# k projections of two heads as one 128-row matmul, and a projection buffer of two single banks, in a fused attention and feed-forward kernel

## The chip, the cores and the metric

The kernel runs on one core of a Trainium2 chip. The metric is the device time of one execution in microseconds (us). The engines are TensorE (PE; its weight loads are listed as PEld), VectorE (DVE), ScalarE (ACT), GpSimd (POOL) and SyncE (SP), which here issues all DMAs in one queue. PSUM, where matmuls write, has eight banks; a bank holds 512 float32 per partition.

## The reference

Linear attention with an exponential feature map, and a two-layer feed-forward network (FFN) on its result, all in float32:

```python
batch, n_heads, seq, head_dim = (8, 8, 576, 64)      # d_feat = 128
def phi(x):
    proj = np.einsum('bhsd,df->bhsf', x, w_phi)
    proj = proj - np.max(np.abs(proj), axis=-1, keepdims=True)
    return np.concatenate([np.exp(proj), np.exp(-proj)], axis=-1)
q_p, k_p = (phi(q), phi(k))
kv = np.einsum('bhsf,bhsd->bhfd', k_p, v)
z = np.sum(k_p, axis=2)
num = np.einsum('bhsf,bhfd->bhsd', q_p, kv)
den = np.einsum('bhsf,bhf->bhs', q_p, z)[..., None] + 1e-06
x = (num / den)                                       # 8 x 576 = 4608 tokens of 512
h = x @ w_in                                          # 512 x 2048
g = 0.5 * h * (1.0 + erf(h * inv_sqrt2))
return g @ w_out                                      # 2048 x 512
```

## The kernel before, in words

The program does not write its instructions down in the order in which they run. Each function calls `op(...)` with an engine, a cost, the buffers read and written, and a rank; `Plan.order` then plays the engines against each other by these costs, takes on each engine the ready operation of lowest rank, and keeps track of buffer slots, activation tables, DMA and PE's clock; `emit` issues everything in the order of the planned starts. So a changed cost, a changed number of slots or a changed kind moves instructions on all engines. On the chip every engine works off its own queue in that order and waits by semaphores. For PE, `SHAPE` says which kinds of matmul use the array in the same division ("f" FFN, "k", "q" projections, "v" kv sums, "n", "d" numerators), and `BEHIND` and `BEFORE` are the costs at a change of division.

**Attention.** Eight batches. `k_quad(b, g, ...)` treats four heads: two pairs of head rows are stacked on 128 partitions (kt), 576 keys of the two pairs lie in nine chunks of 128 columns. The chunks go in five units, of 2, 2, 1, 2 and 2. For each unit, PE projects the chunk (pk): a matmul for each half of 64 partitions, each 64 rows by 128 columns, into the two banks of the pk tile. DVE takes the largest absolute value (mx) and subtracts it in place, ACT makes both exponentials (ek), and PE adds the products with v (vt) in kv, which ACT copies to kvn. `q_pair` projects half a sequence of two heads (pq, two matmuls with 64 rows), ACT copies it (pc), POOL reduces over partitions (mb), DVE subtracts, ACT makes the exponentials (ef), PE makes the numerators (pn), ACT copies them (xo), and DMA writes them to memory (x_d). For batches 0 and 1 the denominators come from PE as a 65th column; for the others DVE (un) and POOL (db) form them. `quotients` makes the reciprocals (dc).

**Buffers in PSUM.** `PS = dict(pp=1, kv=1, pn=1, ph=2, po=1)`: pp is one slot of two banks for pk and, from batch 2 on, for pq. The first two batches (`EB`) take pk from pp and po in turn (`EARLY_PK`) and pq from ph.

**Weights.** 32 tiles of w_in and w_out arrive as 64-bit floats; DMA, two ACT and five DVE instructions for each make of it a high and a low float (raw, wt, w).

**FFN.** 18 blocks of 256 tokens. DMA fetches x_d (xr) and the reciprocals (rb), DVE makes xr, xh and xl; eight steps u each make 24 matmuls with 256 columns (ph), two Gelu on ACT (gh, ph), a difference on DVE (gl) and 12 matmuls with 512 columns (po). Gelu and the exponential need different activation tables, so ACT loads a table when it changes between them.

The planner holds the FFN back until `TF = 90`. After the first block has started, PE works on FFN steps and on attention of later batches in turn.

Of the kernel before, what the change touches and what calls it, by code (L numbers as in the profile page):

```python
# [58 lines left out]
class Plan:
# [19 lines left out]
    def op(self, eng, cost, fn, r=(), w=(), also=(), rank=0.0, table=None, late=0.0, kb=0, duty=1.0, kind="f"):  # L79
        o = Op()  # L80
        o.eng, o.cost, o.fn, o.rank, o.table, o.late, o.n = eng, cost, fn, rank, table, late, len(self.ops)
        o.users, o.ready, o.nbytes, o.duty, o.kind = [], self.since, kb, duty, kind
# [20 lines left out]
        return o

    def order(self, bias):
# [162 lines left out]
def fused_kernel(ctx: ExitStack, tc: tile.TileContext, qT, kT, va, w_st, w_in, w_out, out):  # L268
# [17 lines left out]
    def mm(*a, **kw):  # L286
        return tc.keep_in_program_order(nc.tensor.matmul(*a, **kw))  # L287
# [78 lines left out]
    def k_quad(b, g, kvs, rank):  # L366
# [18 lines left out]
        for u, (p, cs) in enumerate(units):  # L385
            n = len(cs)
            mx = sb["mx"]([P, 2, n], F32, f"mx_{nm}_{u}")
            x = ps[EARLY_PK[turn[0] % len(EARLY_PK)] if b < EB else "pp"]([P, 2, 512], F32, f"pk_{nm}_{u}")
# [8 lines left out]
            xs = lambda x=x, n=n: x()[:, :, : n * NF].rearrange("p j (i f) -> p j i f", i=n)  # L397

            def proj(x=x, cs=cs):
                return [mm(x()[:, j, i * NF : (i + 1) * NF], lhsT=kt()[64 * j : 64 * j + 64, c * P : (c + 1) * P], rhs=wst()[64 * j : 64 * j + 64],  # L400
                           start=True, stop=True) for i, c in enumerate(cs) for j in range(2)]
# [3 lines left out]
                out=mx(), in_=xs(), axis=AX.X, op=ALU.max, apply_absolute_value=True), r=[x], w=[mx], **k())  # L405
            tt("dve", dve(256 * n, True), xs, xs, lambda mx=mx, n=n: mx().unsqueeze(3).to_broadcast([P, 2, n, NF]), ALU.subtract, [x, mx], [x], **k())
            for s in (1, 0):
                op("act", act(256 * n, True), lambda xs=xs, es=es, s=s: nc.scalar.activation(  # L408
                    es[s](), xs(), AF.Exp, scale=1.0 - 2.0 * s), r=[x], w=[e[s]], table="exp", **k())
# [129 lines left out]
    def block(j, rank):  # L539
# [25 lines left out]
        for u in range(NU):  # L565
# [101 lines left out]
def _layout(q, k, v, w_phi, moe_w_in, moe_w_out):  # L667
# [32 lines left out]
```

## Time and profile before

| what | value |
|---|---|
| time, median of 3 runs | 1154.89 us (1153.27 to 1155.93) |
| the profiled execution | 1153.51 us, span 1151.7 us, mean granted clock of PE 0.991 |
| PE busy / weight loads | 1111.6 us (97%) / 914.0 us |
| DVE / ACT / POOL busy | 483.5 / 588.9 / 318.2 us |
| matmuls: records of pk, pq, kv, pn | 576, 256, 2560, 512 |
| matmuls: records of ph, po | 3456, 1728 |

The span runs from the first to the last instruction; the execution's own time is 1.8 us longer. A float32 matmul of the attention leaves two records, one of the FFN leaves one. In rows of a timeline, the first number is the start in the span, the second the length of a merged piece, "x8" the number of records, and "64*128" the rows and columns of the array that are in use. "<-" names what ended an engine's idle time.

### The profile page before, as it was taken

The numbers are of one execution on the slowest core, as the hardware profiler recorded it, in microseconds if no ns is written. First come the engines' busy times: TensorE is split into PE (matmuls) and PEld (weight loads), VectorE is DVE, ScalarE is ACT, GpSimd is POOL, SyncE is SP. The second block draws the span as 40 slices with busy tenths as digits, with TensorE's granted clock in tenths as the row PEclk, the third lists the DMA queues.
The fourth block names the chain that finished last, engine by engine and source line by source line (L and its number), as shares of the span: only waits on it lengthen the run. The fifth ranks groups of instructions, "written<-read, shape, count | busy, mean of one in ns | idle before, by whom it ended". The sixth has DMA issues, their size and how long they took to land.

```text
span 1151.7 us, 21761 instructions
## 1 busy us (share of the span) xinstructions
PE 1111.6 (97%) x9096; PEld 914.0 (79%) x9096; DVE 483.5 (42%) x807; ACT 588.9 (51%) x979; POOL 318.2 (28%) x116
## 2 busy tenths in 40 slices
PE   7887899999999999999999999999999999999998
PEld 4544677787787788788878778789898998989997
DVE  5999796344443534444354444432112212122010
ACT  5877586666684776658476675632121222122121
POOL 3323026345452635445263534430000000000000
PEclk8999999999999999999999999999999999999999
DMA  7667631313212041312213121112012021010000
GB/s 264 200 203 239 185 92 53 98 58 108 63 58 83 29 111 34 123 63 70 72 31 113 33 63 37 58 31 56 11 46 55 1 55 39 18 38 19 1 19 19
DMA packets 73939, 84.92 MB, mean 74 GB/s; under 512 B 23968, under 2 KB 60992, under 8 KB 73840
## 3 DMA queue, kind: packets, MB, share of 16 engines
q1 hardware_dynamic: 73840, 83.52, 24.3%
q8 instruction: 71, 1.16, 0.4%
q14 instruction: 28, 0.23, 0.1%
HBM read 64.32 MB, written 19.17 MB: 72 GB/s over the span
## 4 chain that ended last, share of the span: by engine, by line
PE 85%; DVE 7%; DMA 3%; ACT 2%; issue 1%; SPq 1%; POOL 0%; ACTq 0%; DVEq 0%; POOLq 0%
PE po L287 34%; PE ph L287 34%; PE kv L287 6%; PE pn L287 5%; PE pk L287 3%; PE pq L287 3%; DMA dc<-d_d 1%; DVE mx L404 1%; DVE pk L311 1%; DMA vt<-in_va_dram 1%; ACT ek L408 1%; DVE wt_o L331 1%; PE spin L287 1%; DMA x_d<-xo 1%; DVE w_i L311 0%
## 5 line engine op out<-in xcount | busy, mean ns | idle before, releaser
L287 PE MATMUL ph<-xh,w_i 128*128 128x256 f32 x2304 | 429.3, 282 | 0.0
L287 PEld LDWEIGHTS ph<-xh,w_i 128*128 128x128 f32 x2304 | 359.7, 188 | 13.5 <-issue 5.4
L287 PE MATMUL po<-w_o,gh 128*128 128x512 f32 x1152 | 366.9, 400 | 0.0
L287 PE MATMUL ph<-xl,w_i 128*128 128x256 f32 x1152 | 321.2, 279 | 0.0
L311 DVE TENSOR_TENSOR gl<-ph,gh 128x512 fp32r<-128x512 f32 x144 | 99.4, 690 | 386.5 <-ACT ph L583 385.7
L287 PEld LDWEIGHTS po<-w_o,gh 128*128 128x128 f32 x1152 | 207.5, 188 | 56.8 <-issue 9.9
L287 PE MATMUL po<-w_o,gl 128*128 128x512 f32 x576 | 227.8, 395 | 4.2 <-DVE gl L311 4.2
L460 POOL PARTITION_ALL_REDUCE mb<-pc x64 | 142.2, 2222 | 303.6 <-ACT pc L305 258.1
L582 ACT ACTIVATE gh<-ph 128x512 fp32r<-128x512 f32 x144 | 86.3, 599 | 272.6 <-PE ph L287 272.0
L287 PEld LDWEIGHTS ph<-xl,w_i 128*128 128x128 f32 x1152 | 216.5, 188 | 3.3
L495 POOL PARTITION_ALL_REDUCE db<-un x48 | 176.9, 3686 | 140.8 <-DVE un L492 136.5
L287 PEld LDWEIGHTS po<-w_o,gl 128*128 128x128 f32 x576 | 108.4, 188 | 31.1 <-DVE gl L311 5.8
L287 PEld LDWEIGHTS kv<-vt,ek 128*64 128x64 f32 (+1 forms) x2560 | 86.3, 141 | 41.6 <-ACT ek L408 18.0
L287 PE MATMUL pn<-ef,kvn 128*64 128x288 f32 (+1 forms) x512 | 98.8, 427 | 13.2 <-ACT xo L305 13.1
L287 PE MATMUL kv<-vt,ek 128*64 128x65 f32 (+1 forms) x2560 | 98.4, 229 | 13.3 <-ACT ek L408 11.7
L408 ACT ACTIVATE ek<-pk 128x512 f32<-128x512 f32 (+1 forms) x160 | 80.0, 553 | 41.4 <-DVE pk L311 40.6
L466 ACT ACTIVATE ef<-pc 128x576 f32<-128x576 f32 x128 | 83.1, 684 | 24.0 <-DVE pc L311 23.5
L583 ACT ACTIVATE ph<-ph 128x512 f32<-128x512 f32 x144 | 85.5, 594 | 0.0
L311 DVE TENSOR_TENSOR pc<-pc,mb 128x576 f32<-128x576 f32 x64 | 50.5, 790 | 83.1 <-POOL mb L460 83.1
L582 ACT ACT_TABLE_LOAD x55 | 70.6, 1283 | 19.6 <-PE ph L287 18.9
L404 DVE TENSOR_REDUCE mx<-pk 128x4 f32<-128x512 f32 (+1 forms) x80 | 50.5, 633 | 70.9 <-PE pk L287 70.9
L287 PEld LDWEIGHTS pn<-ef,kvn 128*64 128x64 f32 (+1 forms) x512 | 39.3, 138 | 45.4 <-ACT xo L305 17.1
(41 smaller groups left out, 702.3 us busy)
## 6 DMA issues: line engine op xcount, KB each, us to landing
vt<-in_va_dram SPq DMA_DIRECT2D x16, 585.0 KB
qt<-in_qT_dram SPq DMA_DIRECT2D x64, 144.0 KB
kt<-in_kT_dram SPq DMA_DIRECT2D x16, 576.0 KB
out_dram<-ob SPq DMA_DIRECT2D x36, 256.0 KB
raw_i<-in_w_in_dram SPq DMA_DIRECT2D x16, 512.0 KB
raw_o<-in_w_out_dram SPq DMA_DIRECT2D x16, 512.0 KB
x_d<-xo SPq DMA_DIRECT2D x48, 144.0 KB
x_d<-xo SPq DMA_DIRECT2D x32, 72.0 KB
```

The costliest lines, as they stand in the source:

```text
L287: return tc.keep_in_program_order(nc.tensor.matmul(*a, **kw))
L311: op(eng, cost, lambda: e.tensor_tensor(out=dst(), in0=a(), in1=b(), op=o), r=r, w=w, **kw)
L331: op("dve", dve(512), lambda: v.scalar_tensor_tensor(out=t(), in0=low(), scalar=29, in1=t(), op0=ALU.logical_shift_right, op1=ALU.bitwise_ ...
L404: op("dve", dve(256 * n, True), lambda xs=xs, mx=mx: nc.vector.tensor_reduce(out=mx(), in_=xs(), axis=AX.X, op=ALU.max, apply_absolute_val ...
L408: op("act", act(256 * n, True), lambda xs=xs, es=es, s=s: nc.scalar.activation(es[s](), xs(), AF.Exp, scale=1.0 - 2.0 * s), r=[x], w=[e[s] ...
L460: op("pool", 2.2, lambda mb=mb, pc=pc: nc.gpsimd.partition_all_reduce(mb(), pc(), P, bass_isa.ReduceOp.absmax), r=[pc], w=[mb], **k(1))
L466: op("act", act(2 * HS), lambda ef=ef, pc=pc, s=s: nc.scalar.activation(ef()[:, s], pc(), AF.Exp, scale=1.0 - 2.0 * s), r=[pc], w=[ef], ta ...
L495: op("pool", 3.7, lambda db=db, un=un: nc.gpsimd.partition_all_reduce(db(), un(), P, bass_isa.ReduceOp.add), r=[un], w=[db], **k())
L582: op("act", act(2 * TB, True) + 0.016, lambda gh=gh, ph=ph: nc.scalar.activation(gh(), ph(), AF.Gelu), r=[ph], w=[gh], table="gelu", rank= ...
L583: op("act", act(2 * TB, True) + 0.037, lambda ph=ph: nc.scalar.activation(ph(), ph(), AF.Gelu), r=[ph], w=[ph], table="gelu", rank=URGE + rk)
```

## The change

A chunk of k is projected by one matmul. The weight tile wst becomes a 128 by 256 block matrix, with the weights in the upper left and the lower right block and zeros elsewhere, so that 128 rows of kt and 256 columns give both heads at once. The pk tile becomes one bank, with a chunk in each half, and pp gets two slots. The kind "k" has the shape of "f" in the planner and no cost before it. A pq of batches from 2 on takes both slots, a bank for each head, and two ACT copies as in the early batches. `EARLY_PK` becomes three turns. The planner also adds .9 us (`BLOCKED`) to a DVE operation without PSUM operands, once for each planned POOL operation that it overlaps. `KB = 0` and `HOLD2 = 0.0` leave a second way of subtracting the maximum and a later release of batches unused; the tile mx is twice as wide for it.

```diff
-    BEFORE = {"f": 0.0, "k": 0.09, "q": 0.09, "v": 0.09, "n": 0.09, "d": 0.09}
-    SHAPE = {"f": 0, "k": 1, "q": 1, "v": 2, "n": 2, "d": 3}
+    BEFORE = {"f": 0.0, "k": 0.0, "q": 0.09, "v": 0.09, "n": 0.09, "d": 0.09}
+    SHAPE = {"f": 0, "k": 0, "q": 1, "v": 2, "n": 2, "d": 3}
...
+            if o.eng == "dve" and not o.psum:
+                for span in taken[-4:]:
+                    if t < span[1] - 0.3 and t + cost > span[0] + 0.3 and not span[2]:
+                        span[2] = True
+                        cost += BLOCKED
+            if o.eng == "pool":
+                taken.append([t, t + cost, False])
...
-    PS = dict(pp=1, kv=1, pn=1, ph=2, po=1)
+    PS = dict(pp=2, kv=1, pn=1, ph=2, po=1)
...
-    wst = fixed([P, NF], F32, "wst")
-    op("sp", 0.06, lambda: nc.sync.dma_start(out=wst(), in_=w_st), w=[wst], kb=66, rank=-400.0)
+    wst = fixed([P, 2, NF], F32, "wst")
+    op("sp", 0.06, lambda: nc.sync.dma_start(out=wst(), in_=w_st.rearrange("r (j f) -> r j f", j=2)), w=[wst], kb=131, rank=-400.0)
...
-            x = ps[EARLY_PK[turn[0] % len(EARLY_PK)] if b < EB else "pp"]([P, 2, 512], F32, f"pk_{nm}_{u}")
+            x = ps[EARLY_PK[turn[0] % len(EARLY_PK)] if b < EB else "pp"]([P, 2, 2, NF], F32, f"pk_{nm}_{u}")
...
-                return [mm(x()[:, j, i * NF : (i + 1) * NF], lhsT=kt()[64 * j : 64 * j + 64, c * P : (c + 1) * P], rhs=wst()[64 * j : 64 * j + 64],
-                           start=True, stop=True) for i, c in enumerate(cs) for j in range(2)]
+                return [mm(x()[:, i], lhsT=kt()[:, c * P : (c + 1) * P], rhs=wst(), start=True, stop=True) for i, c in enumerate(cs)]
...
-            if b < EB:
-                pqs = [ps["ph"]([P, HS], F32, f"pq_{nm}_{j}") for j in range(2)]
-                of = [lambda t=t: t() for t in pqs]
-            else:
-                pqs = [ps["pp"]([P, 2, 512], F32, f"pq_{nm}")]
-                of = [lambda j=j, t=pqs[0]: t()[:, j, :HS] for j in range(2)]
+            pqs = [ps["ph" if b < EB else "pp"]([P, HS], F32, f"pq_{nm}_{j}") for j in range(2)]
+            of = [lambda t=t: t() for t in pqs]
...
-            if b < EB:
-                for j in range(2):
-                    copy("act", act(HS, True), lambda pc=pc, j=j: pc()[:, j], of[j], [pqs[j]], [pc], **k(1))
-            else:
-                copy("act", act(2 * HS, True), pc, lambda t=pqs[0]: t()[:, :, :HS], pqs, [pc], **k(1))
+            for j in range(2):
+                copy("act", act(HS, True), lambda pc=pc, j=j: pc()[:, j], of[j], [pqs[j]], [pc], **k(1))
...
-EARLY_PK = ("pp", "po")
+EARLY_PK = ("pp", "pp", "po")
+BLOCKED = 0.9
+HOLD2 = 0.0
+KB = 0
...
-    w_st = np.concatenate([w_phi, w_phi], axis=0)
+    w_st = np.zeros((P, 2, NF), w_phi.dtype)
+    w_st[:D, 0] = w_st[D:, 1] = w_phi
+    w_st = w_st.reshape(P, 2 * NF)
```

The planner's order changes from the first microseconds on, on every engine. Two places:

DVE, where the input of the first FFN block is made (xr, xh, xl), before. This is row 167 to 171 of DVE's queue; w_i and w_o are the last step of a weight tile, wt the steps ahead of it.

```order
L404 TENSOR_REDUCE mx_0_0_1374<-pk_0_0_1358 128x4
L327 TENSOR_SCALAR wt_o_1356<-wt_o_1356 128x512
L311 TENSOR_TENSOR pk_0_0_1358<-pk_0_0_1358,mx_0_0_1374 128x2x256
L329 TENSOR_SCALAR wt_o_1356<-wt_o_1356 128x512
L311 TENSOR_TENSOR pc_3_1_1350<-pc_3_1_1350,mb_3_1_1371 128x576
L331 SCALAR_TENSOR_TENSOR wt_o_1356<-raw_o_1064,wt_o_1356 128x512
L311 TENSOR_TENSOR xr_1214<-xr_1214,rb_1216 128x1024
L333 SCALAR_TENSOR_TENSOR wt_o_1356<-raw_o_1064,wt_o_1356 128x512
L307 CAST xh_1431<-xr_1214 128x1024
L327 TENSOR_SCALAR wt_o_1381<-wt_o_1381 128x512
L311 TENSOR_TENSOR xl_1441<-xr_1214,xh_1431 128x1024
```

Now it is row 142 to 146; 15 weight tiles are finished ahead of it instead of 20, and two k units more.

```order
L319 TENSOR_TENSOR pc_3_0_1246<-pc_3_0_1246,mb_3_0_1267 128x576
L319 TENSOR_TENSOR pk_0_2_1285<-pk_0_2_1285,mx_0_2_1293 128x256
L319 TENSOR_TENSOR w_o_1295<-wt_o_1157,w_o_1295 128x512
L319 TENSOR_TENSOR w_o_1305<-wt_o_1191,w_o_1305 128x512
L319 TENSOR_TENSOR xr_1202<-xr_1202,rb_1204 128x1024
L319 TENSOR_TENSOR pc_3_1_1334<-pc_3_1_1334,mb_3_1_1344 128x576
L315 CAST xh_1400<-xr_1202 128x1024
L335 TENSOR_SCALAR wt_o_1348<-wt_o_1348 128x512
L319 TENSOR_TENSOR xl_1409<-xr_1202,xh_1400 128x1024
L411 TENSOR_REDUCE mx_0_3_1416<-pk_0_3_1396 128x4
```

The weight steps that stood ahead of it have moved behind it.

PE, in the middle of the program, where the last k unit of four heads is projected between kv sums and FFN, before:

```order
L287 MATMUL kv_1_1_4504<-vt_1_3469,ek_1_3_0_4483 64x65 x2
L287 MATMUL kv_1_1_4504<-vt_1_3469,ek_1_3_1_4473 64x65 x2
L287 MATMUL pk_1_4_4531<-wst,kt_1_3428 128x128 x4
L287 MATMUL ph_1_4538<-xh_3661,w_i_0_257 128x256
L287 MATMUL ph_1_4538<-xl_3665,w_i_0_257 128x256
```

And such a place now:

```order
L295 MATMUL kv_1_1_4168<-vt_1_3273,ek_1_3_0_4103 64x65 x2
L295 MATMUL kv_1_1_4168<-vt_1_3273,ek_1_3_1_4086 64x65 x2
L295 MATMUL pk_1_4_4198<-wst,kt_1_3185 128x256 x2
L295 MATMUL pk_0_0_4201<-wst,kt_0_3652 128x256 x2
L295 MATMUL po_4041<-w_o_738,gh_1_4120 128x512 x2
L295 MATMUL po_4041<-w_o_738,gl_1_4140 128x512
```

Four matmuls of a unit have become two, and the first unit of the next four heads stands right behind, in the other slot.

More of the change, by code (lines that the diff above doesn't have):

```diff
@@ L55 @@
 class Op:
-    __slots__ = ("eng", "cost", "fn", "bufs", "rank", "table", "late", "deps", "users", "wait", "ready", "start", "end", "n", "names", "nbytes", "duty", "kind")
+    __slots__ = ("eng", "cost", "fn", "bufs", "rank", "table", "late", "deps", "users", "wait", "ready", "start", "end", "n", "names", "nbytes", "duty", "kind", "psum")
 class Plan:
@@ L77, in pool, with op @@
         return lambda shape, dt, name: Buf(self, tag, lambda: pool.tile(shape, dt, tag=tag, name=name, bufs=bufs))
-    def op(self, eng, cost, fn, r=(), w=(), also=(), rank=0.0, table=None, late=0.0, kb=0, duty=1.0, kind="f"):
+    def op(self, eng, cost, fn, r=(), w=(), also=(), rank=0.0, table=None, late=0.0, kb=0, duty=1.0, kind="f", psum=False):
         o = Op()
         o.eng, o.cost, o.fn, o.rank, o.table, o.late, o.n = eng, cost, fn, rank, table, late, len(self.ops)
-        o.users, o.ready, o.nbytes, o.duty, o.kind = [], self.since, kb, duty, kind
+        o.users, o.ready, o.nbytes, o.duty, o.kind, o.psum = [], self.since, kb, duty, kind, psum
         deps = set()
@@ L142, in order @@
         last, first = ["f"], {}
+        taken = []
         def run(t, work, duty):
@@ L386, in k_quad @@
             n = len(cs)
-            mx = sb["mx"]([P, 2, n], F32, f"mx_{nm}_{u}")
-            x = ps[EARLY_PK[turn[0] % len(EARLY_PK)] if b < EB else "pp"]([P, 2, 512], F32, f"pk_{nm}_{u}")
+            mx = sb["mx"]([P, 2, 2 * n], F32, f"mx_{nm}_{u}")
+            x = ps[EARLY_PK[turn[0] % len(EARLY_PK)] if b < EB else "pp"]([P, 2, 2, NF], F32, f"pk_{nm}_{u}")
             if b < EB and EARLY_E[turn[0] % len(EARLY_E)] != "ek":
@@ L396, in k_quad @@
             turn[0] += 1
-            xs = lambda x=x, n=n: x()[:, :, : n * NF].rearrange("p j (i f) -> p j i f", i=n)
+            xs = lambda x=x, n=n: x()[:, :n].rearrange("p i j f -> p j i f")
             def proj(x=x, cs=cs):
-                return [mm(x()[:, j, i * NF : (i + 1) * NF], lhsT=kt()[64 * j : 64 * j + 64, c * P : (c + 1) * P], rhs=wst()[64 * j : 64 * j + 64],
-                           start=True, stop=True) for i, c in enumerate(cs) for j in range(2)]
+                return [mm(x()[:, i], lhsT=kt()[:, c * P : (c + 1) * P], rhs=wst(), start=True, stop=True) for i, c in enumerate(cs)]
             op("pe", n * PAIR_K, proj, r=[kt, wst], w=[x], also=[mx, *e], kind="k", **k())
             op("dve", dve(256 * n, True), lambda xs=xs, mx=mx: nc.vector.tensor_reduce(
-                out=mx(), in_=xs(), axis=AX.X, op=ALU.max, apply_absolute_value=True), r=[x], w=[mx], **k())
-            tt("dve", dve(256 * n, True), xs, xs, lambda mx=mx, n=n: mx().unsqueeze(3).to_broadcast([P, 2, n, NF]), ALU.subtract, [x, mx], [x], **k())
-            for s in (1, 0):
+                out=mx()[:, 0].rearrange("p (j i) -> p j i", j=2), in_=xs(), axis=AX.X, op=ALU.max, apply_absolute_value=True), r=[x], w=[mx], psum=True, **k())
+            if b < KB:
+                op("dve", 0.09, lambda mx=mx: nc.vector.tensor_scalar(
+                    out=mx()[:, 1], in0=mx()[:, 0], scalar1=-1.0, scalar2=None, op0=ALU.mult), r=[mx], w=[mx], **k())
+                for s in (1, 0):
+                    for j in range(2):
+                        for i in range(n):
+                            op("act", act(NF, True), lambda xs=xs, es=es, s=s, j=j, i=i, n=n, mx=mx: nc.scalar.activation(
+                                es[s]()[:, j, i], xs()[:, j, i], AF.Exp, scale=1.0 - 2.0 * s, bias=mx()[:, 1 - s, j * n + i : j * n + i + 1]),
+                               r=[x, mx], w=[e[s]], table="exp", **k())
+            else:
+                tt("dve", dve(256 * n, True), xs, xs, lambda mx=mx, n=n: mx()[:, 0].rearrange("p (j i) -> p j i", j=2).unsqueeze(3).to_broadcast(
+                    [P, 2, n, NF]), ALU.subtract, [x, mx], [x], psum=True, **k())
+            for s in (1, 0) if b >= KB else ():
                 op("act", act(256 * n, True), lambda xs=xs, es=es, s=s: nc.scalar.activation(
@@ L619, in fused_kernel @@
             continue
+        plan.since = HOLD2
         r0 = T0 + (b - 1) * AT - LEAD
```

5 lines of the change are left out of this document (3 added, 2 removed).

## The prediction

> **What bounds the kernel now.** I read the page's totals first, then a table of stretches, then the waits of TensorE (PE) and the timelines of PE and VectorE (DVE).
>
> ```profile
> span 1151.7 us, 21761 instructions
> PE 1111.6 (97%) x9096; PEld 914.0 (79%) x9096; DVE 483.5 (42%) x807; ACT 588.9 (51%) x979; POOL 318.2 (28%) x116
> ```
>
> The table of stretches (length, then PE, weight loads, DVE, ACT, POOL busy, then granted clock, DMA share, GB/s) says where the 3% are:
>
> ```profile
> 0.00:30.00 30.00, 22.31 (x208) 14.34 (x210) 17.10 (x30) 15.50 (x33) 9.48 (x8) 0.89 0.73 256
> 30.00:60.00 30.00, 26.03 (x292) 15.93 (x290) 27.88 (x46) 24.64 (x55) 8.74 (x4) 0.94 0.68 209
> 60.00:90.00 30.00, 23.15 (x250) 13.93 (x251) 27.72 (x50) 22.81 (x51) 8.92 (x4) 0.94 0.70 214
> 90.00:120.00 30.00, 22.78 (x255) 13.68 (x254) 27.84 (x45) 23.41 (x50) 9.91 (x4) 0.95 0.74 230
> 120.00:150.00 30.00, 26.50 (x262) 21.60 (x261) 25.20 (x49) 18.70 (x32) 0.00 (x0) 0.99 0.54 149
> 150.00:183.00 33.00, 28.95 (x219) 21.71 (x218) 31.77 (x49) 24.35 (x38) 13.12 (x5) 0.95 0.35 98
> 183.00:1146.00 963.00, 961.13 (x7619) 812.52 (x7618) 325.97 (x544) 458.37 (x721) 268.01 (x92) 1.00 0.18 51
> ```
>
> From 183 us on PE is busy 961 of 963 us: it alone bounds, and only PE work counts. Before that DVE bounds: 83.4 of the 90 us from 30 to 120, while PE is busy 79% of the first 120. So the change has two prices: PE work behind the first FFN matmul, and the time at which the FFN starts and fills PE.
>
> **The k projections on PE.** Columns are start, length, engine, line, operation and records. A double unit (two chunks of k) in the FFN's stream, one behind the kv sums, and a single unit, before; then three rows of neighbours that are needed below:
>
> ```profile
> 437.83 0.64 PE L287 MATMUL po<-w_o,gh 128*128 128x512 f32 x2
> 438.30 0.39 PE L287 MATMUL po<-w_o,gl 128*128 128x512 f32 x1
> 438.62 0.72 PE L287 MATMUL pk<-wst,kt 64*128 64x128 f32 x8
> 439.26 0.39 PE L287 MATMUL ph<-xh,w_i 128*128 128x256 f32 x1
> 439.49 0.28 PE L287 MATMUL ph<-xl,w_i 128*128 128x256 f32 x1
> 439.60 0.40 PE L287 MATMUL ph<-xh,w_i 128*128 128x256 f32 x2
> 439.84 0.28 PE L287 MATMUL ph<-xl,w_i 128*128 128x256 f32 x1
> ...
> 407.65 1.77 PE L287 MATMUL kv<-vt,ek 64*64 64x65 f32 x48
> 409.34 0.72 PE L287 MATMUL pk<-wst,kt 64*128 64x128 f32 x8
> 409.99 0.39 PE L287 MATMUL ph<-xh,w_i 128*128 128x256 f32 x1
> ...
> 130.95 0.49 PE L287 MATMUL pk<-wst,kt 64*128 64x128 f32 x4
> 131.37 0.73 PE L287 MATMUL po<-w_o,gh 128*128 128x512 f32 x2
> ...
> 121.29 1.19 PE L287 MATMUL pn<-ef,kvn 128*65 128x288 f32 x4
> 122.41 0.71 PE L287 MATMUL pk<-wst,kt 64*128 64x128 f32 x8
> ...
> 416.89 0.76 PE L287 MATMUL pq<-qt,wst 64*128 64x288 f32 x4
> 417.57 0.38 PE L287 MATMUL ph<-xh,w_i 128*128 128x256 f32 x1
> ...
> 427.95 1.19 PE L287 MATMUL pn<-ef,kvn 128*64 128x288 f32 x8
> 429.08 0.73 PE L287 MATMUL po<-w_o,gh 128*128 128x512 f32 x2
> ```
>
> Lengths overlap, so I price by starts. Normal spacing is .235 us for a po record (.47 for two) and .12 for a ph record (.35 for three). The double unit starts .32 behind the last po record (.09 too late), runs .64, and the ph record behind it holds its successor .23 (.11 too long). So a unit costs .65 (.42 when single), and a trip of PE into the 64-row shape and back .09 + .11 = .20. Behind kv sums PE is in a narrow shape already, and pk shares their trip.
>
> Afterwards a chunk is one 128-row matmul with 256 columns. No row has that form. A second pair of 128 columns adds .65 - .42 = .23 to a unit; twice the columns without a partner would be .44 to .46. The 65-column pn matmul (128 rows, 288 columns) takes 1.12/2 = .56 with its shape change, and 256/288 of it is .50: the dear end. The cheap end takes from that the shape's .20 shared by two: (1.12 - .20)/2 x 256/288 = .41. I take .435, nearest to the doubled pair. Against PE's FFN neighbours I price the way in and out at 0, since the shape is theirs; the dear end is .20 for the 10 places where pk follows an FFN matmul, 2 us.
>
> By counting the order behind the first FFN matmul: before there are 46 double and 12 single units, 46 x .65 + 12 x .42 = 34.9 us; the same 104 chunks afterwards 104 x .435 = 45.2, so +10.3. Trips into a narrow shape go from 111 to 63, because k no longer needs one and the planner puts more attention work in a row: 48 x .20 = -9.6. Net +0.7 us (-1.9 at .41, +7.5 at .50). The changed order also does 5 chunks (2.2) and 32 kv matmuls (.07 each by the 48 records in 1.69; 2.2) before the first FFN matmul that now come behind it, and two pn fewer (.6): -4 us behind it.
>
> Against this change speaks the Trainium skill: "TensorEngine Tiling (Array Packing)", section "Theoretical Speedup", promises up to 2x where a dimension of at most 64 is packed in two tiles, and the change gives that packing up. By that rule alone the sum would be some 24 us higher, in place of 0.7; the rows here give most of it back as trips not made.
>
> **Second slot, copies, tables.** The group of k matmuls in the stretch from 183 us, then ACT's groups over the whole span (busy, mean ns | idle before):
>
> ```profile
> L287 PE MATMUL pk<-wst,kt 64*128 64x128 f32 x380 | 35.5, 300 | 0.0
> ...
> L305 ACT COPY pc<-pq 128x576 f32<-128x576 f32 x48 | 30.9, 643 | 40.9 <-PE pq L287 40.9
> L305 ACT COPY pc<-pq 128x288 f32<-128x288 f32 x32 | 11.5, 402 | 8.2 <-PE pq L287 8.2
> L582 ACT ACT_TABLE_LOAD x55 | 70.6, 1283 | 19.6 <-PE ph L287 18.9
> ```
>
> PE never waits there for a free k buffer, so the second slot itself is worth 0. One 643 ns copy becomes two of 402: 48 x .16 = 7.7 us more on ACT, hidden by ACT's 458 of 963 us; uncovered they cost those 7.7. The order holds 88 table loads instead of 110, 22 x 1.28 = 28 us less on ACT, hidden too. The weight tile's DMA doubles from 64 to 128 KB, beside the spin matmuls at the start:
>
> ```profile
> 2.27 6.47 PE L287 MATMUL spin<-idle 128*128 128x512 f32 x8 [2.27 <-ACT idle L292]
> ```
>
> They end at 8.7 us, so I take 0, at most the extra 64 KB at the 256 GB/s of the first stretch, .3 us.
>
> **When the FFN starts.** Here the gain or loss is decided. First DVE instruction on k, then the last one ahead of the FFN, the first FFN matmul, the first and sixth gl of block 0:
>
> ```profile
> 9.91 0.69 DVE L404 TENSOR_REDUCE mx<-pk 128x4 f32<-128x512 f32 x1 [8.53 <-PE pk L287]
> ...
> 121.56 1.22 DVE L311 TENSOR_TENSOR xl<-xr,xh 128x1024 fp32r<-128x1024 f32 x1
> ...
> 123.86 0.49 PE L287 MATMUL ph<-xh,w_i 128*128 128x256 f32 x1
> ...
> 129.76 0.69 DVE L311 TENSOR_TENSOR gl<-ph,gh 128x512 fp32r<-128x512 f32 x1
> ...
> 177.49 0.61 DVE gl L311
> ```
>
> In the old order 170 DVE instructions from that first one end with xl at 122.8: 112.9/170 = .66 us each. In the new order 145 do: 29 weight instructions are put off and 4 on k come forward. By DVE alone the FFN starts 25 x .66 = 16.5 us sooner, at 107.4. But PE now has more to do before it: 40 chunks at .435 instead of .325 (4.4), the 4 us from above, and some 20 returns to full shape for k, x .20 (4): +12. By starts PE's work there was 32 pq x .34 + 64 pn x .56 + 336 kv x .07 + 40 chunks x .325 = 83 us, and becomes 95; its first such matmul stands at 8.7, so without any wait the FFN starts at 104. Its waits in the first 120 us:
>
> ```profile
> PE pn L287 <- ACT xo L305: 12.2, 10, 2.9
> PE kv L287 <- ACT ek L408: 8.9, 9, 2.2
> ```
>
> If these 21 us stay, the start is at 125, no sooner than now. They hang on exponentials and copies that come late because DVE works off weights in between; with 29 of those fewer I take half: 114. Ends: 106 (DVE's 107, less a little) and 126.
>
> From the first gl to the first gl of block 1 the new order has 130 DVE instructions. The old one took 47.7 us for 70, so 130 take 89; 20 of them are the short ones on un, and I take 86. So that gl comes at start + 6 + 86. PE has meanwhile 228 ph (.117), 96 po (.235), 112 kv (.07), 22 pn (1.13/4), 13 chunks and 10 pq (.34) and a dozen trips: 74. It waits 18 us, where before it waited 3.5 + 4.05 + 1.9 = 9.5 behind the FFN's start.
>
> Sum: before, 1151.7 - 123.9 = 1027.8 behind the start. After, 1027.8 + 0.7 - 4 + 18 - 9.5 = 1033, and 114 + 1033 = 1147 us of span: -4.7. The profiled execution took 1153.51 (1.8 beside its span) and so becomes 1149; the median of the runs is 1.4 above it, so 1150.
>
> **Rivals.** What this kernel's measurement tells from no change is about 0.2%, 2.3 us.
> - PE paces the early stage (slower). Place: PE between 9 and 124 us. The doubled columns and the returns for k land on an engine whose work, at these prices, now stands some 5 us ahead of DVE's at each early k unit of the order, and its waits for ACT stay. It decides from a start at 121 us; at 126 the sum is 1159 of span, 1162 by the median. For it: 95 us of PE work from 8.7 to 114 need 0.9 of the time, and no row before the FFN shows PE above 26.03 of 30. Against: DVE, busy 93%, loses 29 instructions there.
> - No difference: start between 117 and 121, gain and extra cost cancel.
> - PE waits behind 183 us (slower). q now takes both slots, so k behind q waits for two copies; 48 pairs x .4 (the second copy) = 19 us, 1170. Against: PE waited under 2 us in 963 with one slot, and the planner sees the slots.
> - The doubled streaming counts in full and no trip is saved: 104 chunks x (.65 - .42) = 24 us in place of 0.7, 1173. Against: the .09 and .11 stand in the rows. The tiling page of the Trainium skill, taken alone, is this rival.
>
> **How the numbers follow.** Forecast .56, no difference .16, PE paces .18, waits behind 183 .06, doubled streaming .04. The predicted time is the forecast's, 1150; its own range, by starts from 106 to 117, is 1142 to 1153. The range must take in the first two rivals: 1141 (1142 for a start at 106, less part of the 2.6 us that .41 a chunk would save) to 1162. Faster .56, within 0.2% .16, slower .28.
>
> **What would show it.** First FFN matmul near 114 us, PE busy above 26 of 30 in the early rows and again nearly all of the time from some 205 us on; k matmuls as 128-row records .22 apart, no .09 and .11 around them in the FFN's stream; DVE idle early where it was full; fewer table loads. I am wrong if the FFN starts at 121 or later, if PE shows waits behind 210 us, or if a chunk takes .50.

## The result and the profile after

The changed kernel takes 1164.75 us (median of 5 runs, 1160.88 to 1167.11) against 1153.66 (1153.12 to 1155.93) of the kernel before beside it: ratio 1.0095, 95% interval 1.0075 to 1.0114. I had forecast 1150 within 1141 to 1162, so both the sign and the range were wrong. The profiled execution took 1164.75 us, its span 1163.0.

The page's totals, and the table of stretches with the columns of before:

```profile
span 1163.0 us, 21189 instructions
PE 1123.4 (97%) x8808; PEld 934.4 (80%) x8808; DVE 505.2 (43%) x807; ACT 561.7 (48%) x1005; POOL 319.2 (27%) x116
```

```profile
0.00:30.00 30.00, 26.10 (x233) 15.69 (x234) 18.94 (x29) 18.75 (x42) 10.43 (x9) 1.00 0.84 289
30.00:60.00 30.00, 27.63 (x324) 17.63 (x323) 27.17 (x46) 24.02 (x54) 7.32 (x4) 1.00 0.65 204
60.00:90.00 30.00, 26.03 (x251) 15.80 (x248) 24.80 (x45) 21.17 (x48) 9.80 (x4) 0.94 0.74 217
90.00:120.00 30.00, 26.02 (x252) 17.43 (x251) 23.51 (x36) 21.38 (x48) 8.59 (x4) 0.94 0.78 234
120.00:150.00 30.00, 25.94 (x202) 19.48 (x201) 25.64 (x45) 20.73 (x37) 11.33 (x4) 1.00 0.55 169
150.00:183.00 33.00, 24.07 (x194) 19.08 (x192) 32.00 (x53) 20.18 (x33) 14.09 (x4) 0.96 0.11 30
183.00:210.00 27.00, 25.97 (x214) 22.42 (x216) 24.25 (x41) 19.49 (x34) 3.38 (x2) 0.80 0.19 55
210.00:720.00 510.00, 503.05 (x4348) 409.54 (x4345) 252.20 (x417) 320.39 (x540) 254.25 (x87) 1.00 0.25 71
```

PE is fuller up to 120 us than before (26 of 30), and has two holes: 150 to 210 us, where it is idle for 10 of 60 us and its clock falls to .80, and 210 to 720, where it is idle for 7 us. In the kernel before that stretch reads, with less on DVE:

```profile
210.00:720.00 510.00, 508.55 (x4597) 408.96 (x4596) 223.04 (x401) 331.46 (x503) 232.50 (x80) 1.00 0.23 68
```

The same 807 DVE instructions of the program take 505.2 us in place of 483.5. One form has most of it, pc (the subtraction of the maximum that POOL formed). Its group in the whole span, after, and then before:

```profile
L319 DVE TENSOR_TENSOR pc<-pc,mb 128x576 f32<-128x576 f32 x64 | 64.4, 1006 | 77.8 <-POOL mb L472 77.6
```

```profile
L311 DVE TENSOR_TENSOR pc<-pc,mb 128x576 f32<-128x576 f32 x64 | 50.5, 790 | 83.1 <-POOL mb L460 83.1
```

The timelines of POOL, DVE, ACT and PE at one such place in the kernel after (start, length):

```profile
274.49 2.26 POOL L472 PARTITION_ALL_REDUCE mb<-pc  x1 [1.51 <-DVE pc L319]
276.66 3.67 POOL L507 PARTITION_ALL_REDUCE db<-un  x1
...
273.58 0.75 DVE L319 TENSOR_TENSOR pc<-pc,mb 128x576 f32<-128x576 f32 x1
...
276.79 3.09 DVE L319 TENSOR_TENSOR pc<-pc,mb 128x576 f32<-128x576 f32 x1 [0.57 <-POOL mb L472]
...
279.91 0.68 ACT L478 ACTIVATE ef<-pc 128x576 f32<-128x576 f32 x1 [4.29 <-DVE pc L319]
280.50 1.05 ACT L313 COPY ob<-po 128x512 f32<-128x512 f32 x2
281.44 0.69 ACT L478 ACTIVATE ef<-pc 128x576 f32<-128x576 f32 x1
282.03 0.40 ACT L313 COPY xo<-pn 128x288 f32<-128x288 f32 x1
...
282.48 1.19 PE L295 MATMUL pn<-ef,kvn 128*64 128x288 f32 x8 [1.34 <-ACT xo L313]
```

A pc takes .75 us while POOL does nothing and 3.09 us while POOL sums db. ACT waits 4.29 us for it, the copy of pn behind it comes at 282.03, and PE, which needs that one slot of pn, stands still for 1.34 us. The kernel before has one pc that long, the kernel after seven.

### The profile page after: what moved, and what is told of

It reads as the page before. It is cut to its first block, busy times and chain, and to the rows that moved or that the text cites. A ratio compares the mean times of both kernels' runs of the same rounds, so it can differ in the third digit from the quotient of the medians.

```text
span 1163.0 us, 21189 instructions
## 1 busy us (share of the span) xinstructions
PE 1123.4 (97%) x8808; PEld 934.4 (80%) x8808; DVE 505.2 (43%) x807; ACT 561.7 (48%) x1005; POOL 319.2 (27%) x116
## 4 chain that ended last, share of the span: by engine, by line
PE 77%; DVE 9%; DMA 4%; ACT 4%; POOL 2%; issue 2%; SPq 1%; ACTq 0%; DVEq 0%; POOLq 0%
PE ph L295 31%; PE po L295 31%; PE kv L295 5%; PE pn L295 4%; PE pk L295 4%; PE pq L295 2%; DMA dc<-d_d 2%; DVE pc L319 2%; POOL mb L472 1%; DMA x_d<-xo 1%; DVE wt_i L339 1%; ACT ef L478 1%; DVE mx L411 1%; ACT ek L427 1%; DVE wt_i L337 1%
## 5 line engine op out<-in xcount | busy, mean ns | idle before, releaser
L295 PE MATMUL ph<-xl,w_i 128*128 128x256 f32 x1152 | 324.7, 282 | 0.0
L295 PEld LDWEIGHTS po<-w_o,gh 128*128 128x128 f32 x1152 | 210.2, 188 | 50.9 <-ACT gh L594 3.2
L507 POOL PARTITION_ALL_REDUCE db<-un x48 | 178.5, 3718 | 155.1 <-DVE un L504 116.3
L295 PE MATMUL pn<-ef,kvn 128*64 128x288 f32 (+1 forms) x512 | 96.4, 422 | 11.6 <-ACT xo L313 9.0
L295 PE MATMUL kv<-vt,ek 128*64 128x65 f32 (+1 forms) x2560 | 95.7, 226 | 6.2 <-ACT ek L427 6.1
L319 DVE TENSOR_TENSOR pc<-pc,mb 128x576 f32<-128x576 f32 x64 | 64.4, 1006 | 77.8 <-POOL mb L472 77.6
L295 PE MATMUL pk<-wst,kt 128*128 128x256 f32 x288 | 75.1, 393 | 1.8 <-ACT pc L313 1.8
```

What stands on the lines that cost most here:

```text
L319: op(eng, cost, lambda: e.tensor_tensor(out=dst(), in0=a(), in1=b(), op=o), r=r, w=w, **kw)
L507: op("pool", 3.7, lambda db=db, un=un: nc.gpsimd.partition_all_reduce(db(), un(), P, bass_isa.ReduceOp.add), r=[un], w=[db], **k())
```

## How lost time is counted

To compare kernels whose orders differ, I priced every matmul of PE's order by the spacing of starts (ph .117, po .232, kv .059, pn 1.12 for eight records, a double unit of k .645 before and .863 after, trips .093 in and .105 out; pq and the 65-column pn as in the prediction) and subtracted the work that stands ahead of an FFN matmul from its start in the trace. What is left is lost: waits, a slow clock, and matmuls that start further apart than they are priced. These columns are estimates from the traces' starts. "Stretch" adds up by how much DVE instructions behind 203 us exceed their usual duration, where that is more than .25 us. Work, lost time and some 5 us behind the last FFN matmul make the span. "PE waits behind" adds up PE's idle pieces of more than .15 us behind 203 us. "ph spacing" is the mean distance behind 203 us between the starts of two ph records that follow each other (distances of .16 us and more left out). Times are medians, the rest comes from the profiled execution of each.

| kernel | median us | PE work | lost by 203 us | lost behind | stretch | PE waits behind | ph spacing, ns |
|---|---|---|---|---|---|---|---|
| before | 1153.7 | 1099.0 | 47.9 | -0.3 | 10.3 | 1.9 | 116.1 |
| e4: before, BLOCKED .9 | 1148.1 | 1098.0 | 38.1 | 3.7 | 17.5 | 4.3 | 116.3 |
| e10: before, BLOCKED 2.3 | 1163.9 | 1099.4 | 54.7 | 1.4 | 18.2 | 1.8 | 116.8 |
| e1: before, block matmul | 1159.0 | 1114.3 | 37.8 | 0.2 | 11.3 | 0.4 | 116.7 |
| e2: e1, shape told | 1162.8 | 1113.4 | 37.2 | 4.5 | 12.0 | 2.9 | 116.7 |
| e8: e2, BLOCKED .9 | 1160.5 | 1114.7 | 34.6 | 3.0 | 20.0 | 3.1 | 116.7 |
| after | 1164.8 | 1107.7 | 39.2 | 11.5 | 31.7 | 6.9 | 118.0 |
| e3: after, BLOCKED 0 | 1170.1 | 1107.3 | 46.1 | 10.7 | 28.0 | 5.1 | 118.0 |
| e9: after, two early turns | 1155.0 | 1106.3 | 30.2 | 11.4 | 31.5 | 5.2 | 118.0 |
| e11: e9, BLOCKED 0 | 1172.5 | 1108.6 | 35.6 | 20.6 | 31.4 | 11.2 | 117.9 |
| e12: e9, BLOCKED 2.3 | 1175.4 | 1103.2 | 55.0 | 10.6 | 29.1 | 4.3 | 118.0 |
| e13: after, later release | 1167.5 | 1111.1 | 41.9 | 9.1 | 25.7 | 4.3 | 118.0 |
| e14: e9, later release | 1154.5 | 1110.5 | 30.1 | 6.3 | 15.8 | 2.0 | 118.0 |
| e15: e11, later release | 1177.8 | 1109.5 | 36.9 | 24.7 | 28.9 | 14.1 | 118.0 |
| e7: before, short sum | 1147.3 | 1099.0 | 42.6 | -1.5 | 3.7 | 1.1 | 116.2 |
| e6: after, short sum | 1150.3 | 1107.7 | 29.6 | 5.4 | 3.8 | 1.5 | 118.0 |
| e16: e11, short sum | 1155.4 | 1108.6 | 35.0 | 7.5 | 2.2 | 2.6 | 118.0 |
| e17: e15, short sum | 1155.3 | 1109.5 | 32.7 | 7.1 | 1.9 | 2.9 | 118.0 |

The change in this count: PE work +8.7, lost by 203 us -8.7, lost behind 203 us +11.8; the span grew by 11.3. e12's row needs care. The stage of the weights lasts there until some 212 us, so part of its late loss belongs there: PE waits only .2 us behind 300 us. And it has the same matmuls and about as many changes of shape as e9 (279 and 281), so its work should be near 1106, not 1103.

The +11.8 has two parts; what they leave, under 1 us, is within the error of the prices. PE's waits behind 203 us rose from 1.9 to 6.9 us, by 5.0. From 210 to 1140 us they are, before and then after:

```profile
PE kv L287 <- ACT ek L408: 1.4, 1, 1.4
PE po L287 <- DVE gl L311: 0.4, 1, 0.4
```

```profile
PE po L295 <- DVE gl L319: 3.5, 3, 2.1
PE pn L295 <- ACT xo L313: 3.4, 3, 1.3
```

The other part is no wait. With some 3250 ph records behind 203 us, 118.0 ns in place of 116.1 are 6 us in which PE is busy. A row of ph records behind the attention, before and then after (33 records from the first line's start to the last line's):

```profile
1002.06 0.28 PE L287 MATMUL ph<-xl,w_i 128*128 128x256 f32 x1
...
1005.82 0.28 PE L287 MATMUL ph<-xl,w_i 128*128 128x256 f32 x1
```

```profile
1001.47 0.28 PE L295 MATMUL ph<-xl,w_i 128*128 128x256 f32 x1
...
1005.36 0.28 PE L295 MATMUL ph<-xl,w_i 128*128 128x256 f32 x1
```

These take 3.76 us, .114 a record, and 3.89 us, .118 a record, both at a granted clock of 1.00. Before, such rows of 36 or 48 records run at about .1136 or at .1187; after, at .1172 to .1194. All ten kernels with two slots have 117.9 or 118.0 ns, all eight with one slot 116.1 to 116.8. Those with two slots differ in other things too (pk tiles of one bank, a wider mx), and no run shows what sets the spacing.

## The experiments

In the expectations, A says that the loss is PE work of the block matmul and DVE instructions held by POOL; B that it comes with the two slots of one bank and the waits of their order; C that the planner's cost BLOCKED made it; D that it is an accident of each order.

**The parts, added one by one.** e1 is the kernel before with the block matrix and the block matmul alone ("..." stands for lines left out):

```diff
-                return [mm(x()[:, j, i * NF : (i + 1) * NF], lhsT=kt()[64 * j : 64 * j + 64, c * P : (c + 1) * P], rhs=wst()[64 * j : 64 * j + 64],
-                           start=True, stop=True) for i, c in enumerate(cs) for j in range(2)]
+                return [mm(x()[:, i, : 2 * NF], lhsT=kt()[:, c * P : (c + 1) * P], rhs=wst(), start=True, stop=True) for i, c in enumerate(cs)]
...
```

> The kernel before with the block matrix and the one-matmul chunk alone: one slot of two banks, a chunk in each bank, the planner's numbers and so every instruction's place as before. Theory A (the change adds PE work, and what the earlier FFN start brings is given back where DVE instructions are stretched by POOL): PE work behind the first FFN matmul grows by 7 us by the prices of a chunk and of the trips, the 8 us ahead of it hide behind DVE, so +6 to +9 us against before. Theory B (the two single-bank slots, which q takes both, make PE wait late): within 2 us of before. Theory C (the planner's new cost for a DVE instruction beside POOL makes a worse order): within 2 us of before.

1159.02 us, ratio 1.0043 [1.0029, 1.0057]: +4.8 against the kernel before at its side, a little under A's range, and outside that of B and C. The form costs by itself: 15.3 us more PE work, of which 10.1 disappear in time that was lost early anyway.

e2 also tells the planner that k has the FFN's shape:

```diff
-    BEFORE = {"f": 0.0, "k": 0.09, "q": 0.09, "v": 0.09, "n": 0.09, "d": 0.09}
-    SHAPE = {"f": 0, "k": 1, "q": 1, "v": 2, "n": 2, "d": 3}
+    BEFORE = {"f": 0.0, "k": 0.0, "q": 0.09, "v": 0.09, "n": 0.09, "d": 0.09}
+    SHAPE = {"f": 0, "k": 0, "q": 1, "v": 2, "n": 2, "d": 3}
```

> As the form alone, and the planner is told that k has the FFN's shape; still one slot of two banks, no cost for POOL. Theory A: PE work behind the first FFN matmul is 10.6 us above before by the same prices, and DVE collides with POOL about as often as before (some 24 us of stretch), so +8 to +12 us. Theories B and C: within 2 us of before.

1162.77 us, 1.0072 [1.0049, 1.0096]: +8.5, as A expected. Almost no work is saved by it (-.9), and 4.3 us more are lost late.

e3 is the kernel after without the cost of an overlap with POOL, e4 the kernel before with that cost and nothing else:

```diff
-BLOCKED = 0.9
+BLOCKED = 0.0
```

> The changed kernel with the planner's cost for a DVE instruction beside POOL set to 0: block matmul, shape and two slots stay. Theory A: PE work in all 8 us above before, early idle as before (the order finishes 19 weight tiles ahead of the FFN as against 20 before and 15 after), so +6 to +11 us. Theory B: as the changed kernel, +10 or more, with PE waits of about 8 us behind 250 us. Theory C: within 3 us of before.

> The kernel before with only the planner's cost for a DVE instruction beside POOL added. Theory A: PE work is 1 us less, the order starts the FFN sooner (17 weight tiles ahead of it instead of 20), collisions decide; between -6 and +3 us. Theory B: within 2 us of before. Theory C: +8 us or more, as in the changed kernel.

e3 1170.13 us, 1.0128 [1.0109, 1.0148]; e4 1148.06 us, .9938 [.9913, .9962]. The cost helped in both, so C falls as far as these two go. e3 is 15.9 us above the kernel before at its side, more than A's +6 to +11, and where B had put it; e4's -6.2 is just past the end of A's range. e4 is faster than both kernels of this case.

e8 is the kernel after with one slot of two banks, the old tiles of pk, pq and mx, and the old two early turns; e9 the kernel after with the old early turns and its two slots. The second hunk is in both:

```diff
-    PS = dict(pp=2, kv=1, pn=1, ph=2, po=1)
+    PS = dict(pp=1, kv=1, pn=1, ph=2, po=1)
...
-EARLY_PK = ("pp", "pp", "po")
+EARLY_PK = ("pp", "po")
```

> Block matmul, shape and the planner's cost for a DVE instruction beside POOL, but one slot of two banks: the changed kernel without its two slots. If the parts add up (form +5, shape +3, POOL's cost -4 to -6 as seen on either side): +2 to +4 us against before, and no PE waits behind 210 us. By theory A, which puts the late waits on collisions that the new order makes, they could stay: +10. By theory B (slots): +2 to +4.

> The changed kernel with the first two batches taking pk from pp and po in turn, as before, instead of pp, pp, po. PE work in all is 1.4 us less by the prices, and 2 us more of it is ahead of the first FFN matmul. If the third turn in the early stage is worth something, the FFN starts later than at 116.6 us and the time is 3 us or more above the changed kernel; theory B of the late waits expects them to stay, 8 us or more behind 210 us.

e8 1160.51 us, 1.0048 [1.0031, 1.0066]; e9 1154.97, 1.0008 [.9991, 1.0024]. Two slots save 8.4 us of PE work (1114.7 to 1106.3) because units of k stand side by side, and lose 8.4 us behind 203 us, 2.1 of it in PE's waits and some 4 in the spacing of ph. e8, at +6.9, lies between what A and B expected, with the small late loss of B; in e9 the late loss stayed, as B expected. e9's first FFN matmul comes later than that of the kernel after (121.7 us in place of 116.6), as expected, and it is still the faster one. By e9 the third early turn alone would cost 9.8 us. The next three say that this is not a price of the turn.

> The kernel before with the planner's cost for a DVE operation that overlaps a POOL operation, 2.3 us instead of .9 (about 3.09 - .79, what the longest stretched pc instructions lost); nothing of k is changed. Theory A (the loss of the changed kernel is PE work, DVE instructions held by POOL, and the third early turn): with .9 the kernel before gained 5.6 us, and DVE's stretched instructions still cost 33 us in it, 17.5 of them behind 203 us; a dearer overlap in the plan should take some of these away: 1142 to 1148 us. Rival D (the .9 gained by an order that happened to start the FFN at 114 us, not by fewer overlaps): no further gain, 1147 to 1156 us.

> The changed kernel with two early turns (pp, po) and the cost of an overlap with POOL 0 instead of .9: form, shape and two slots of one bank alone. Theory A with additive parts: 1155.0 with .9, and the .9 was worth 4 to 6 us in two other pairs and 2 in a third, so 1157 to 1161 us; the two slots then are worth 2 to 6 us against one slot (1162.8). Rival B (two slots alone make late waits): 1163 to 1170 us.

> The changed kernel with two early turns and the cost of an overlap with POOL 2.3 instead of .9. Theory A: the late waits of PE behind 203 us (11 us in it with .9) are held DVE instructions, and fewer overlaps in the plan make them fewer: 1147 to 1154 us. Rival D (the cost only reshuffles the order): 1153 to 1160 us.

e10 1163.91 us, 1.0083 [1.0054, 1.0113]; e11 1172.45, 1.0164 [1.0142, 1.0186]; e12 1175.40, 1.0177 [1.0151, 1.0202]. All three missed what A expected; D's ranges for e10 and e12 were missed as well, and B's for e11 by 2.5 us. The third turn costs 9.8 us with BLOCKED .9 (e9 to after) and gains 2.3 with 0 (e11 to e3). BLOCKED from 0 to .9 gains 5.6 (before to e4), 2.3 (e2 to e8), 5.4 (e3 to after) and 17.5 us (e11 to e9); from .9 to 2.3 it loses 15.9 and 20.4. Parts that set an order do not add up. Two columns of the table depend on the order little: PE work (1098 to 1099 with the old form, 1113 to 1115 with one slot and the new, 1106 to 1111 with two, but for e12), and the loss behind 203 us, under 5 us in all six kernels with one slot and a full sum, over 9 in all five with two slots so far. Some 4 to 6 us of that step are the spacing of ph; PE's waits alone are .4 to 4.3 us with one slot and 4.3 to 11.2 with two. The loss by 203 us goes from 30 to 55 us and is what the orders deal out.

**Is it the POOL sum?** e6 and e7 are the kernels after and before with the sum over partitions that makes the denominators (db) taken over 32 columns in place of 576 for each head, and written out repeated, so their output is not the reference's. The order stays.

```diff
-            op("pool", 3.7, lambda db=db, un=un: nc.gpsimd.partition_all_reduce(db(), un(), P, bass_isa.ReduceOp.add), r=[un], w=[db], **k())
+            op("pool", 3.7, lambda db=db, un=un: nc.gpsimd.partition_all_reduce(db()[:, 0, :32], un()[:, 0, :32], P, bass_isa.ReduceOp.add), r=[un], w=[db], **k())
...
```

> The changed kernel, in which POOL's sum for the denominators of batches 2 to 7 (db) is made over 32 columns instead of 576 and written out repeated, so the output is not the reference's; every instruction keeps its place. It takes away most of POOL's time in which DVE can be held up. Theory A (the late PE waits are DVE instructions held up by that POOL work): DVE's stretched time falls from 49 us by 20 or more, the pc instructions of 3.09 us behind 143 us go, PE's waits behind 203 us fall from 11 us to under 4: 7 to 12 us faster than the changed kernel, 1153 to 1158. Theory B (the slots themselves make PE wait for copies): within 3 us of the changed kernel.

> The same shortening of POOL's sum in the kernel before (the output is not the reference's). PE waits nowhere behind 200 us there, so by theory A it gains only what the stretch of 150 to 200 us holds: 0 to 4 us faster than before. By theory B 0 as well; it is the yardstick for the run above.

e6 1150.25 us, .9963 [.9943, .9983], 14.5 less than the kernel after (A expected 7 to 12, B at most 3); e7 1147.33, .9922 [.9898, .9947], 6.3 less than the kernel before at its side. The late loss of the kernel after halves: PE's waits behind 203 us fall from 6.9 to 1.5 us, while the spacing of ph stays at 118.0 ns. By 203 us it loses 9.6 us less. The kernel before gains too, more than the 0 to 4 us that I expected; its gain lies ahead of 203 us but for 1.2.

**Is it the density?** With two slots the attention runs denser: the last k starts at 630 us (717 before), and from 203 us to POOL's last instruction POOL is busy .55 of the time (.46). e13, e14 and e15 hold batches from 4 on to the pace of the kernel before, with two slots kept. PE's order ahead of batch 4, up to some 285 us, stays.

```diff
+            if b > 3:
+                plan.since = 212.0 + 103.0 * (b - 3) + 51.5 * g
```

> The changed kernel, with the batches of attention from 4 on released by the planner at 315, 418, 521 and 624 us (half a batch 51.5 us later), about when the kernel before projects their first k, instead of 285, 375, 464 and 539; the order up to batch 4 stays as it is. Theory B' (two slots let the planner run the attention some 100 us denser: the last k at 630 us instead of 717, POOL busy .55 of the time from 203 us to its last instruction instead of .46, so more DVE instructions are held and PE waits for gl and xo): PE's waits behind 300 us, 8.8 us, fall to 2 or less; PE's work grows by 3.4 us (fewer units side by side), so 1157 to 1162 us in place of 1164.75. Rival D (the waits are an accident of each order and have nothing to do with the density): the waits stay and the work is added, 1166 to 1170 us.

> The changed kernel with two early turns (1155.0 us), and the same later release from batch 4 on. Theory B': the waits behind 300 us, 10.0 us, fall to 2 or less, the work grows by 4.2: 1147 to 1153 us. Rival D: 1157 to 1161 us.

> The changed kernel with two early turns and a cost of an overlap with POOL of 0 (1172.45 us), and the same later release from batch 4 on. Here PE waited most behind 300 us, 18.3 us. Theory B': they fall to 3 or less, the work grows by .9: 1154 to 1162 us. Rival D: 1170 to 1176 us.

e13 1167.53 us, 1.0125 [1.0109, 1.0141]; e14 1154.54, 1.0015 [1.0001, 1.0028]; e15 1177.79, 1.0213 [1.0197, 1.0229]. e13 lies in D's range, e14 between the two, e15 above both. POOL's share fell to .45, .45 and .44, yet the loss behind 300 us went only from 8.8 to 6.2, from 10.0 to 4.9, and in the third from 18.3 up to 22.1. The expectations call all of that loss waits; the waits in the trace there went from 4.8 to 2.2, from 4.7 to 1.4, and from 9.6 to 12.4 us. Density is not the cause by itself. e14, the one with less stretch (15.8 us), has the least late loss of the kernels with two slots.

e13 shows something else. PE's order is that of the kernel after up to batch 4, and still its first FFN matmul came at 122.4 us, not 116.6:

```profile
90.00:120.00 30.00, 25.07 (x219) 15.67 (x220) 20.65 (x31) 19.39 (x44) 8.59 (x4) 0.80 0.76 219
```

The clock stood at .80 in this stretch, .94 in the kernel after: 4 us of 30. So single profiles of the early stage carry that much chance.

**The worst two with a short sum.** e16 and e17 are e11 and e15 with the sum over 32 columns, as above.

> The changed kernel with two early turns and a cost of an overlap of 0 (1172.45 us; PE waited 20.6 us behind 203 us, the second most of all), with the sum over partitions that gives the denominators (db) on POOL over 32 columns instead of 576; the output is then not the reference's, and all instructions and their order stay. Theory A (the late waits come from DVE instructions held while POOL sums): the 31 us of stretched DVE instructions behind 203 us fall to about 4 as in the other two kernels with a short sum, the waits to 6 or less: 1150 to 1160 us. Rival D (the waits are those of the order, DVE's stretch only stands beside them): 1166 to 1173 us.

> The same with the later release of the batches from 4 on (1177.79 us with the full sum; PE waited 24.7 us behind 203 us, the most of all, although the attention was as thin as before the change). The denominators' sum is over 32 columns, so the output is not the reference's. Theory A: the waits fall to 7 or less, 1154 to 1164 us. Rival D: 1171 to 1179 us.

e16 1155.42 us, 1.0010 [.9992, 1.0028]; e17 1155.26, .9995 [.9973, 1.0017]: 17.0 and 22.5 us less, as A expected; D expected 0 to 7. By 203 us they lose what they lost before to within .6 and 4.2, and behind it 13.1 and 17.6 us less. PE's waits behind 203 us fall from 11.2 to 2.6 and from 14.1 to 2.9 us. PE's waits in e11 from 210 to 1140 us (total, count, longest), then in e16:

```profile
PE po L295 <- DVE gl L319: 4.7, 7, 1.1
PE pn L295 <- ACT ef L478: 2.2, 1, 2.2
PE pn L295 <- ACT xo L313: 1.9, 2, 1.6
PE pk L295 <- ACT pc L313: 0.8, 2, 0.6
PE pq L295 <- ACT ek L427: 0.4, 1, 0.4
```

```profile
PE pk L295 <- ACT pc L313: 0.6, 1, 0.6
PE po L295 <- DVE gl L319: 0.5, 1, 0.5
PE pn L295 <- ACT xo L313: 0.4, 1, 0.4
```

And DVE's groups pc and xh from 210 to 720 us, in e11 and then in e16:

```profile
L319 DVE TENSOR_TENSOR pc<-pc,mb 128x576 f32<-128x576 f32 x44 | 44.7, 1016 | 69.1 <-POOL mb L472 69.1
...
L315 DVE CAST xh<-xr 128x1024 fp32r<-128x1024 f32 x7 | 10.6, 1518 | 7.3 <-PE ph L295 7.3
```

```profile
L319 DVE TENSOR_TENSOR pc<-pc,mb 128x576 f32<-128x576 f32 x44 | 33.1, 753 | 81.7 <-POOL mb L472 81.7
...
L315 DVE CAST xh<-xr 128x1024 fp32r<-128x1024 f32 x7 | 4.9, 695 | 12.5 <-PE ph L295 12.5
```

With the sum short, pc falls back to 753 ns, xh from 1518 to 695, and the waits for gl, ef and xo fall from 8.8 to .9 us. A short sum also ends sooner, so DVE no longer waits for db's single slot before the next un. That wait does not go with the late loss: from 203 to 800 us DVE waited 58.6 us for it in e10, which lost 1.4 us late, and 39.8 in e8, which lost 3.0; the kernel after waited 26.7 and lost 11.5. So I hold the stretch to be the larger part, but the runs do not split the two: they show that POOL's long sum makes most of PE's late waits, not by which way. Stretch alone does not give the waits either. e12 has 29.1 us of it behind 203 us, yet PE waits only 4.3 us there, .2 of it behind 300 us.

## Why the prediction was wrong, point by point

**A chunk of k at .435 us: right.** Rows of the kernel after, three chunks among FFN matmuls, then two:

```profile
299.04 0.28 PE L295 MATMUL ph<-xh,w_i 128*128 128x256 f32 x1
299.16 1.46 PE L295 MATMUL pk<-wst,kt 128*128 128x256 f32 x6
300.26 0.47 PE L295 MATMUL ph<-xh,w_i 128*128 128x256 f32 x1
300.57 0.28 PE L295 MATMUL ph<-xl,w_i 128*128 128x256 f32 x1
...
248.89 0.39 PE L295 MATMUL po<-w_o,gl 128*128 128x512 f32 x1
249.12 1.02 PE L295 MATMUL pk<-wst,kt 128*128 128x256 f32 x4
249.79 0.83 PE L295 MATMUL po<-w_o,gh 128*128 128x512 f32 x2
```

pk starts .23 behind a po record and .12 behind a ph record, the normal spacing, so there is no way in. Three chunks hold from 299.16 to 300.26, and the ph behind them holds its successor .31 in place of .12: 1.10 + .19 = 1.29, .43 for each. Way in and out cost 0, as taken.

**PE work: right.** +12 ahead of the first FFN matmul and -3.3 behind it were forecast, +8.7; by the table's count it is +11.9 and -3.2. Against the Trainium skill, "TensorEngine Tiling (Array Packing)", section "Theoretical Speedup" (up to 2x where a dimension of at most 64 is packed): e1 shows the packing given up with one slot kept, +15.3 us of PE work for all 144 chunks, where the rival's .23 a chunk would give 33, because some trips fall away; with two slots 8.7. The rival that rested on it mis-sized the work. Its time, 1173, lies near that of e11 by chance: e11's work is 1108.6, and its time comes from lost time.

**The start of the FFN: nearly right.**

```profile
115.87 1.13 PE L295 MATMUL pn<-ef,kvn 128*65 128x288 f32 x4
116.62 0.49 PE L295 MATMUL ph<-xh,w_i 128*128 128x256 f32 x1
```

116.6 us against 114 forecast, 2.6 lost. PE's waits ahead of it were halved, as I took: 12.2 and 8.9 before,

```profile
PE kv L295 <- ACT ek L427: 6.1, 4, 3.1
PE pn L295 <- ACT xo L313: 5.6, 6, 2.4
```

So the rival in which PE paces the early stage, from a start at 121 us, fell too, though it named 1162.

**Waits in block 0: mis-sized by 2.0 us.** I took 18 us in place of 9.5, +8.5. The loss from the first FFN matmul to 203 us is 20.9 in place of 10.4, +10.5. The weights that had been put off are what PE stood for, and then the clock fell:

```profile
177.20 0.28 PE L295 MATMUL ph<-xh,w_i 128*128 128x256 f32 x1
182.14 0.58 PE L295 MATMUL ph<-xh,w_i 128*128 128x256 f32 x1 [4.66 <-ACT w_i L313]
182.52 0.42 PE L295 MATMUL ph<-xl,w_i 128*128 128x256 f32 x1
182.97 0.58 PE L295 MATMUL ph<-xh,w_i 128*128 128x256 f32 x1
184.34 0.58 PE L295 MATMUL ph<-xh,w_i 128*128 128x256 f32 x1 [0.79 <-ACT w_i L313]
```

A ph matmul took .28 alone before that wait and .42 after it. The clock of .80 over 27 us is 5.4 us of work, an estimate, which the forecast had no term for. That the wait of 4.7 us brought the slow clock on is read from their order in this one trace, not tested.

**"PE is busy nearly all of the time from some 205 us on": the step that failed.** I priced waits behind 203 us at 0, "the second slot itself is worth 0", and carried the FFN's own matmuls over at their old spacing in the 1027.8 us. The loss there is 11.5 us (before -0.3): +11.8, as much as the whole slowdown. Added to my -4.7 the three errors make -4.7 + 2.6 + 2.0 + 11.8 = +11.7; the span shows +11.3.

Two terms that I put at nothing are in it. PE's waits grew by 5.0 us. I had seen in the row that PE waited for no k buffer, and took the slot for idle. But a second slot lets the planner start units of k and pairs of q earlier and side by side, and in this order DVE's pc, xr and xh fell onto POOL's sums: 31.7 us of stretch in place of 10.3. With the short sum the waits fall to 1.5 us. Rows with pc at 790 ns mean and single ones at .75 were there to be read in the profile of before; I took DVE's durations as fixed. The other 6 us are ph records that start 118.0 ns apart in place of 116.1; here PE is busy, as I had said, and still slower.

The sign hangs on the order as well. e9 has the same late loss (11.4 us) and takes 1155.0 us, no longer than the kernel before, because it lost 9.0 us less than the kernel after by 203 us.

**What hid, hid.** Table loads are 88, as counted; the second copy of pc delayed PE once, 1.8 us ahead of 210, and not behind it. So the rival of waits for q's two slots (1170) fell by its mechanism.

**Left open.** Why DVE falls onto POOL's sums more with two slots than with one, with the attention as thin as before (e13, e15). Why ph records lie 118.0 ns apart with two slots; this is most of the 5 to 8 us that are lost late with a short sum and two slots. And the loss by 203 us, which differs by 25 us among these orders: I can name its waits in each, not forecast them.

## What to carry to other kernels

Where a planner sets the order, price the matmul work, which the order gives to a microsecond, apart from lost time, which it does not; test a setting in more than one order before it is given a price. A DVE duration is not fixed while POOL works: ask of every change what it moves beside POOL's sums, even where DVE is busy only 43%. A buffer for which nobody waits can still cost, because it lets work move. And look whether the instructions that a change leaves alone kept their spacing: 2 ns for each of some 3250 matmuls made half of what the late loss grew by here.

## What the runs showed of the hardware

A DVE subtraction of two 128x576 tensors, .75 us alone, took 3.09 us beside POOL's sum of 3.67. The Trainium skill, "SBUF — State Buffer", section "SBUF: two separate sides", says that a DVE operation with two SBUF inputs and a GpSimd operation that reads SBUF take a shared pair of ports for the whole instruction, and that the loser blocks. The trace agrees that it is held, and differs in the end: this pc ended at 279.88, and the sum that held it at 276.66 + 3.67 = 280.33, though POOL's spans are rough. xh, a cast with one input, was held too: 1518 ns mean in e11, 695 in e16.

The same ph matmul, at a granted clock of 1.00, starts on average 113.6 or 118.7 ns behind the one ahead of it in the rows of ph records behind the attention of the kernel before, and 117.2 to 119.4 in those of the kernel after. The pattern repeats from block to block; the cause is not shown.
